# Layer one of a token-pair MLP: both halves of a pair accumulated in one PSUM bank

## The chip, the cores and the metric

The kernel runs on one core of a Trainium2 chip. The metric is the device time of one execution in microseconds (us); three runs of the kernel before are given. The engines in the text are TensorE (PE in the profile, its weight loads PEld), VectorE (DVE), ScalarE (ACT), GpSimd (POOL) and the DMA queue of SyncE (SP).

## The reference

A two-dimensional Fourier transform, of which the real part is kept, followed by two MLPs on the 6016 rows of 256 values:

```
X = fft(fft(x, axis=1), axis=2).real          # x: 2 x 3008 x 256
t = X.reshape(6016, 256)
h = t @ w_in;   t = silu(h) @ w_out           # 256 -> 2048 -> 256
h = t @ w2_in;  out = h * clip(h + 3, 0, 6) / 6 @ w2_out
```

## The kernel before

The real part of the transform at token k and at token -k have the same even part and the opposite odd part over the 256 columns. The kernel therefore works on 3010 pairs: the transform leaves `eo`, an even part (128 rows) and an odd part (128 rows) of each pair, in columns. Layer one multiplies the even part by the folded even weights and the odd part by the folded odd weights; the sum of the two products is the hidden value of one token of the pair, their difference that of the other. Row 0 of the odd part is free of a weight of its own; it holds the value of column 128, the Nyquist term, which enters both tokens alike, and is added by VectorE as `eb` (that row copied to all partitions through DRAM) times `w128_sb`.

All products are of float32 values cut into a high and a low part, three matmuls each (`mm3`, lines 242 to 245): 128 x 128 weights, 502 columns. Layer one runs over six chunks of 502 pairs and sixteen blocks `f` of 128 hidden values, in two passes over the chunks; one chunk and one `f` are a unit, 96 in all, and the first two of them (`EARLY`) are begun while the transform still runs (loop of line 492). Layer two follows with 96 units of its own.

The order on each engine is the order in which the program is written. In the loop of line 597 step i does: `win1` of unit i (six matmuls into the bank pair `ab`; VectorE's reads in lines 471, 474 and 475 make `h`, both tokens), `low` of unit i-1 (GpSimd, line 541: `h` less its high part), `wout1` of unit i-3 (twelve matmuls, line 557, from `ghi` and `glo` into `y00` to `y11`), the low parts of a new chunk that wait in `later` (line 167, `xlo`), and `parts` of unit i (ScalarE, lines 484 and 485: Silu of both tokens, as the high part and in full). Then `spare` lets VectorE go on with other work by a credit of 1150 ns a unit (line 458): the weights arrive as float64 words, and VectorE decodes them in steps (lines 104 to 116, 174 to 180, 142), whose costs in the code are only the credit's counting. `win1` drives this decoder on if the weights of its `f` are not there yet. The last four stretches of that work are the staging of layer two's weights (lines 192 to 202). The bank pair has two buffers, `h` two, `ghi` four, `glo` three.

Of the kernel before, what the change touches and what calls it, by code (L numbers as in the profile page):

```python
# [70 lines left out]
def body(tc, xh, x128, t1, t2, t3, w1, w128, w2, out):  # L71
# [101 lines left out]
    def add_w1(t, a):  # L173
        V.tensor_tensor(out=a[:, :, 0:256], in0=a[:, :, 0:256], in1=t[:, :, 0:256], op=ALU.add)
        yield 680
        V.tensor_tensor(out=t[:, :, 256:512], in0=a[:, :, 256:512], in1=t[:, :, 256:512], op=ALU.add)  # L176
        yield 680
        V.tensor_tensor(out=t[:, :, 0:128], in0=a[:, :, 0:128], in1=a[:, :, 128:256], op=ALU.add)
        yield 420
        V.scalar_tensor_tensor(  # L180
            out=t[:, :, 128:256], in0=a[:, :, 0:128], scalar=mask, in1=a[:, :, 128:256],
            op0=ALU.mult, op1=ALU.subtract,
        )
        yield 420
# [57 lines left out]
    def mm3(o, wh, wl, xhi, xlo, first, last):  # L242
        T.matmul(o, wh, xhi, start=first, stop=False)  # L243
        T.matmul(o, wh, xlo, start=False, stop=False)  # L244
        T.matmul(o, wl, xhi, start=False, stop=last)  # L245
# [274 lines left out]
    def win2(k, f):  # L520
# [4 lines left out]
        hp, h, ghi = hidden_tiles()  # L525
# [71 lines left out]
    for i in range(len(units) + LAG):  # L597
        if i < len(units):
# [176 lines left out]
```

## Time and profile before

| | before |
|---|---|
| median of 3 runs | 989.57 us |
| lowest, highest | 989.51, 989.65 us |
| span of the profiled execution, first to last instruction | 987.7 us |
| mean granted TensorE clock | 0.995 |
| busy: TensorE, VectorE, ScalarE, GpSimd | 972.2, 657.7, 512.3, 234.8 us |

A row of the timeline gives the start in us from the span's start, the duration, the engine, the line, the operation with its output and inputs, and in brackets the idle time of the engine before it and what ended that. Matmuls overlap, so the sum of their durations is more than the time they take; the distance of two starts is what one costs. PEclk is the clock that was granted to TensorE, as a share of 2.4 GHz.

### The profile page before, as it was taken

What the parts mean: (1) busy time and instruction counts of PE and PEld (TensorE: products, weight loads), DVE (VectorE), ACT (ScalarE), POOL (GpSimd) and SP (SyncE); (2) the same over time, 40 slices, a digit from 0 to 9 for tenths busy, and PEclk for the clock granted to TensorE, in tenths of its full rate; (3) what the DMA queues carried; (4) which work ended last, traced back from release to release, by engine and by line L of the source; (5) the groups of instructions that cost most, each with busy time, mean ns of one, the idle gap of its engine ahead of it and who ended that gap; (6) DMA issues with size and microseconds to landing.
All of it is one profiled execution on the core that took longest, in us unless ns stands there. A gap on an engine that the chain in (4) does not pass through costs nothing.

```text
span 987.7 us, 10943 instructions
## 1 busy us (share of the span) xinstructions
PE 972.2 (98%) x4416; PEld 807.9 (82%) x4416; DVE 657.7 (67%) x724; ACT 512.3 (52%) x559; POOL 234.8 (24%) x101
## 2 busy tenths in 40 slices
PE   9979999999899999999999999999999999999998
PEld 8958878888788888888888888888888888888886
DVE  6899999998989765876976455554444444443533
ACT  3867666665465545665555444344443434444442
POOL 0045556565566655552000000000000000000000
PEclk9989999999999999999999999999999999999999
DMA  9411111000212010031100000000000000000000
GB/s 367 170 54 63 54 43 54 11 19 24 75 64 75 23 32 23 31 107 43 43 1 0 1 22 21 21 21 21 0 21 1 21 1 21 11 11 22 1 22 21
DMA packets 11007, 40.46 MB, mean 41 GB/s; under 512 B 1350, under 2 KB 6348, under 8 KB 8140
## 3 DMA queue, kind: packets, MB, share of 16 engines
q1 hardware_dynamic: 10812, 39.49, 11.1%
q8 instruction: 34, 0.56, 0.3%
q10 hardware_dynamic: 144, 0.27, 0.1%
q14 instruction: 17, 0.14, 0.0%
HBM read 31.48 MB, written 8.27 MB: 40 GB/s over the span
## 4 chain that ended last, share of the span: by engine, by line
PE 81%; DVE 13%; issue 3%; ACT 2%; DMA 1%; ACTq 0%; DVEq 0%
PE y L243 14%; PE y L245 14%; PE y L244 14%; PE ab L243 12%; PE ab L245 12%; PE ab L244 12%; DVE h L471 2%; DVE h L474 2%; DVE h L475 2%; DMA x<-in_xh 1%; PE ps L337 1%; PE ps L293 1%; DVE lo L176 1%; DVE wlo L142 1%; DVE lo L116 1%
## 5 line engine op out<-in xcount | busy, mean ns | idle before, releaser
L243 PE MATMUL y<-ghi,whi 128*128 128x502 f32 (+1 forms) x768 | 301.3, 392 | 2.0 <-ACT eo L351 1.7
L245 PE MATMUL y<-ghi,wlo 128*128 128x502 f32 (+1 forms) x768 | 300.7, 392 | 0.0
L244 PE MATMUL y<-glo,whi 128*128 128x502 f32 (+1 forms) x768 | 300.1, 391 | 0.0
L541 POOL TENSOR_TENSOR glo<-h,ghi 128x1004 fp32r<-128x1004 f32 (+1 forms) x96 | 234.4, 2442 | 219.9 <-ACT h L485 191.5
L531 DVE SCALAR_TENSOR_TENSOR h<-h,ab 128x1004 f32<-128x1004 f32 (+1 forms) x96 | 115.2, 1200 | 255.4 <-ACT h L530 255.4
L530 ACT ACTIVATE h<-ab,three 128x1004 f32<-128x1004 f32 (+1 forms) x96 | 105.5, 1099 | 157.0 <-PE ab L245 145.0
L484 ACT ACTIVATE ghi<-h 128x1004 fp32r<-128x1004 f32 (+1 forms) x96 | 100.2, 1044 | 149.8 <-DVE h L475 138.4
L243 PEld LDWEIGHTS y<-ghi,whi 128*128 128x128 f32 x768 | 145.4, 189 | 33.8 <-ACT eo L351 2.4
L244 PEld LDWEIGHTS y<-glo,whi 128*128 128x128 f32 x768 | 145.9, 190 | 30.6
L245 PEld LDWEIGHTS y<-ghi,wlo 128*128 128x128 f32 x768 | 145.2, 189 | 30.2
L482 ACT ACTIVATE ghi<-h 128x1004 fp32r<-128x1004 f32 (+1 forms) x96 | 100.3, 1045 | 125.1 <-DVE h L531 125.1
L243 PE MATMUL ab<-uhi,whi 128*128 128x502 f32 (+1 forms) x384 | 149.9, 390 | 0.0
L245 PE MATMUL ab<-uhi,wlo 128*128 128x502 f32 (+1 forms) x384 | 149.8, 390 | 0.0
L244 PE MATMUL ab<-ulo,whi 128*128 128x502 f32 (+1 forms) x384 | 149.7, 390 | 0.0
L541 DVE TENSOR_TENSOR glo<-h,ghi 128x1004 fp32r<-128x1004 f32 (+1 forms) x96 | 114.9, 1197 | 0.0
L485 ACT ACTIVATE h<-h 128x1004 f32<-128x1004 f32 (+1 forms) x96 | 100.3, 1044 | 9.0 <-ACT ghi L484 0.4
L471 DVE SCALAR_TENSOR_TENSOR h<-eb,w_sb,ab 128x502 f32<-128x502 f32 (+1 forms) x96 | 70.2, 731 | 43.1 <-PE ab L245 38.3
L244 PEld LDWEIGHTS ab<-ulo,whi 128*128 128x128 f32 x384 | 72.6, 189 | 15.2
L243 PEld LDWEIGHTS ab<-uhi,whi 128*128 128x128 f32 x384 | 72.4, 188 | 15.0
L245 PEld LDWEIGHTS ab<-uhi,wlo 128*128 128x128 f32 x384 | 72.2, 188 | 15.0
L243 PE MATMUL ab<-xhi,whi 128*128 128x502 f32 (+1 forms) x192 | 76.1, 396 | 6.2 <-DVE h L475 6.2
L245 PE MATMUL ab<-xhi,wlo 128*128 128x502 f32 (+1 forms) x192 | 75.9, 395 | 1.2 <-DVE wlo L142 1.2
(89 smaller groups left out, 798.8 us busy)
## 6 DMA issues: line engine op xcount, KB each, us to landing
raw<-in_w SPq DMA_DIRECT2D x16, 1024.0 KB, 5.0
x<-in_xh SPq DMA_DIRECT2D x6, 1024.0 KB, 7.0
out<-y SPq DMA_DIRECT2D x20, 251.0 KB, 2.1
eb<-e_d SPq DMA_DIRECT2D x10, 251.0 KB, 3.6
w_d<-ta SPq DMA_DIRECT2D x4, 512.0 KB, 2.9
w<-w_d SPq DMA_DIRECT2D x4, 512.0 KB, 4.1
x<-in_xh SPq DMA_DIRECT2D x3, 512.0 KB
out<-y SPq DMA_DIRECT2D x4, 250.0 KB, 2.0
```

The costliest lines, as they stand in the source:

```text
L243: T.matmul(o, wh, xhi, start=first, stop=False)
L244: T.matmul(o, wh, xlo, start=False, stop=False)
L245: T.matmul(o, wl, xhi, start=False, stop=last)
L471: V.scalar_tensor_tensor(out=h[:, 0, :n], in0=eb[:, :n], scalar=w128_sb[:, f : f + 1], in1=ab[:, 0, :n], op0=ALU.mult, op1=ALU.add)
L474: V.tensor_tensor(out=h[:, 1, :n], in0=h[:, 0, :n], in1=ab[:, 1, :n], op=ALU.subtract)
L475: V.tensor_tensor(out=h[:, 0, :n], in0=h[:, 0, :n], in1=ab[:, 1, :n], op=ALU.add)
L482: A.activation(ghi[:, :, :n], h[:, :, :n], AF.Copy)
L484: A.activation(ghi[:, :, :n], h[:, :, :n], AF.Silu)
L485: A.activation(h[:, :, :n], h[:, :, :n], AF.Silu)
L530: A.activation(h[:, :, :n], hp[:, :, :n], AF.Relu, bias=three)
L531: V.scalar_tensor_tensor(out=h[:, :, :n], in0=h[:, :, :n], scalar=6.0, in1=hp[:, :, :n], op0=ALU.min, op1=ALU.mult)
L541: eng.tensor_tensor(out=glo[:, :, :n], in0=h[:, :, :n], in1=ghi[:, :, :n], op=ALU.subtract)
```

## The change

Layer one's unit is split in two. `win1` now does the even product alone, into one bank (`ab`, four buffers of one bank), and VectorE reads it once: `z` is the bank plus `eb` times `w128_sb`. `win1_end` then accumulates the odd product onto the same bank, without clearing it. The odd weights are folded with the opposite sign, and their row 0 is no longer zero but the weight row 128, so the bank ends as the full hidden value of the second token, Nyquist term included; VectorE computes the first token as twice `z` less the bank. ScalarE takes the second token's Silu from the bank itself. Its two activations over both tokens become four over one each, and GpSimd's subtraction becomes two of half the size. In the loop, step i finishes unit i and then begins unit i+1, both ahead of `low` and `wout1`; a `z` buffer (one) is added. At the start of layer two the pool of the banks is released and a new one of bank pairs is opened. The weight tables follow: `mask` and a new `minus` fold both halves with the same instruction, in place of lines 178 and 180.

```
-        V.tensor_tensor(out=t[:, :, 0:128], in0=a[:, :, 0:128], in1=a[:, :, 128:256], op=ALU.add)
-        V.scalar_tensor_tensor(out=t[:, :, 128:256], in0=a[:, :, 0:128], scalar=mask, in1=a[:, :, 128:256],
-            op0=ALU.mult, op1=ALU.subtract)
+        for o, scalar in ((0, mask), (128, minus)):
+            V.scalar_tensor_tensor(
+                out=t[:, :, o : o + 128], in0=a[:, :, 128 - o : 256 - o], scalar=scalar, in1=a[:, :, o : o + 128],
+                op0=ALU.mult, op1=ALU.add)
+            yield 420
...
     def win1(k, f):
         while len(finished) <= f:
             drive(steps)
-        ab, h, ghi = hidden_tiles()
-        for i in range(2):
-            wh, wl = w(1, f, 128 * i)
-            mm3(ab[:, i, :n], wh, wl, hi[:, i, :n], lo[:, i, :n], True, True)
+        ab = pools[1].tile([P, 512], F32, name="ab", tag="ab")
+        z = pools[0].tile([P, CHUNK], F32, name="z", tag="z", bufs=1)
+        product(ab[:, :n], w(1, f, 0), (hi[:, 0, :n], lo[:, 0, :n]), True)
         V.scalar_tensor_tensor(
-            out=h[:, 0, :n], in0=eb[:, :n], scalar=w128_sb[:, f : f + 1], in1=ab[:, 0, :n], op0=ALU.mult, op1=ALU.add
+            out=z[:, :n], in0=eb[:, :n], scalar=w128_sb[:, f : f + 1], in1=ab[:, :n], op0=ALU.mult, op1=ALU.add
         )
-        V.tensor_tensor(out=h[:, 1, :n], in0=h[:, 0, :n], in1=ab[:, 1, :n], op=ALU.subtract)
-        V.tensor_tensor(out=h[:, 0, :n], in0=h[:, 0, :n], in1=ab[:, 1, :n], op=ALU.add)
-        return h, ghi
+        begun[k, f] = ab, z
+
+    def win1_end(k, f):
+        ab, z = begun.pop((k, f))
+        h, ghi = hidden_tiles()
+        product(ab[:, :n], w(1, f, 128), (hi[:, 1, :n], lo[:, 1, :n]), False)
+        V.scalar_tensor_tensor(
+            out=h[:, 0, :n], in0=z[:, :n], scalar=2.0, in1=ab[:, :n], op0=ALU.mult, op1=ALU.subtract
+        )
+        gs[k, f] = h, ghi, ab
...
-        A.activation(ghi[:, :, :n], h[:, :, :n], AF.Silu)
-        A.activation(h[:, :, :n], h[:, :, :n], AF.Silu)
+        h, ghi, ab = gs[k, f]
+        for s, src in ((1, ab[:, :n]), (0, h[:, 0, :n])):
+            A.activation(ghi[:, s, :n], src, AF.Silu)
+            A.activation(h[:, s, :n], src, AF.Silu)
...
         if g >= 11 and g - 11 < EARLY:
-            k, f = units[g - 11]
-            gs[k, f] = win1(k, f)
-            parts(k, f)
+            win1_end(*units[g - 11])
+            parts(*units[g - 11])
+        if g >= 10 and g - 10 <= EARLY:
+            win1(*units[g - 10])
...
+        if segs[k][0] == 1:
+            for s in (1, 0):
+                G.tensor_tensor(out=glo[:, s, :n], in0=h[:, s, :n], in1=ghi[:, s, :n], op=ALU.subtract)
...
+            if i == n1:
+                pools[1].release()
+                pools[1] = tc.alloc_tile_pool(name="psS", bufs=2, space=PSUM, side="right", reuse_waits="tile")
...
-            if i >= EARLY:
-                gs[k, f] = (win1 if layer == 1 else win2)(k, f)
+                if i >= EARLY:
+                    win1_end(k, f)
+                if EARLY <= i < n1 - 1:
+                    win1(*units[i + 1])
...
-    w1[1:, :, 128:256] = wb[129:256].reshape(P - 1, NF, P)
+    w1[:, :, 128:256] = wb[128:256].reshape(P, NF, P)
```

On TensorE, in the first units, before: `ab_630` is unit 3, both parts, and `y00_644` the start of `wout1` of unit 0.

```order
L243 MATMUL ab_630<-xhi1_530,whi1_0_496 128x502 [waits DVE_49]
L244 MATMUL ab_630<-xlo1_531,whi1_0_496 128x502
L245 MATMUL ab_630<-xhi1_530,wlo1_0_497 128x502
L243 MATMUL ab_630<-xhi1_530,whi1_0_496 128x502
L244 MATMUL ab_630<-xlo1_531,whi1_0_496 128x502
L245 MATMUL ab_630<-xhi1_530,wlo1_0_497 128x502
L243 MATMUL y00_644<-ghi_554,whi1_0_496 128x502 [waits Activation_49]
L244 MATMUL y00_644<-glo_607,whi1_0_496 128x502 [waits Pool_49]
```

Now the even part of unit 3 (`ab_629`), its odd part, the even part of unit 4 (`ab_654`), and then `wout1` of unit 0:

```order
L243 MATMUL ab_629<-xhi1_533,whi1_0_499 128x502
L244 MATMUL ab_629<-xlo1_534,whi1_0_499 128x502
L245 MATMUL ab_629<-xhi1_533,wlo1_0_500 128x502
L243 MATMUL ab_629<-xhi1_533,whi1_0_499 128x502 [waits DVE_49]
L244 MATMUL ab_629<-xlo1_534,whi1_0_499 128x502
L245 MATMUL ab_629<-xhi1_533,wlo1_0_500 128x502
L243 MATMUL ab_654<-xhi1_533,whi1_1_642 128x502 [waits Activation_49]
L244 MATMUL ab_654<-xlo1_534,whi1_1_642 128x502
L245 MATMUL ab_654<-xhi1_533,wlo1_1_643 128x502 [waits DVE_49]
L243 MATMUL y00_663<-ghi_562,whi1_0_499 128x502 [waits PE_49]
L244 MATMUL y00_663<-glo_620,whi1_0_499 128x502 [waits Pool_49]
```

The odd part is a group of its own that waits for VectorE, and a part of unit 4 stands ahead of the first `wout1`.

On VectorE, the same units, before: three reads of `ab` for units 0, 1 and 2, with decode steps of the second weight tile between them.

```order
L471 SCALAR_TENSOR_TENSOR h<-eb_467,w_sb,ab 128x502 [waits DMAHW3_49,PE_49]
L474 TENSOR_TENSOR h<-h,ab 128x502 [waits DVE_49]
L475 TENSOR_TENSOR h<-h,ab 128x502 [waits DVE_49]
L114 TENSOR_SCALAR lo_1_474<-hi_1_473 128x1024
L116 SCALAR_TENSOR_TENSOR lo_1_474<-raw_1_277,lo_1_474 128x1024 [waits DVE_49]
L471 SCALAR_TENSOR_TENSOR h<-eb_467,w_sb,ab 128x502 [waits PE_49]
L474 TENSOR_TENSOR h<-h,ab 128x502 [waits DVE_49]
L475 TENSOR_TENSOR h<-h,ab 128x502 [waits DVE_49]
L174 TENSOR_TENSOR hi_1_473<-hi_1_473,lo_1_474 128x2x256
L176 TENSOR_TENSOR lo_1_474<-hi_1_473,lo_1_474 128x2x256
L178 TENSOR_TENSOR lo_1_474<-hi_1_473 128x2x128 [waits DVE_49]
L180 SCALAR_TENSOR_TENSOR lo_1_474<-hi_1_473,mask 128x2x128
```

Now `h` of one unit and `z` of the next stand together, and the same decode steps (one line number higher) follow:

```order
L484 SCALAR_TENSOR_TENSOR h<-z,ab 128x502 [waits DVE_49,PE_49]
L473 SCALAR_TENSOR_TENSOR z<-eb_470,w_sb,ab 128x502 [waits DVE_49,PE_49]
L115 TENSOR_SCALAR lo_1_477<-hi_1_476 128x1024
L117 SCALAR_TENSOR_TENSOR lo_1_477<-raw_1_280,lo_1_477 128x1024 [waits DVE_49]
L484 SCALAR_TENSOR_TENSOR h<-z,ab 128x502 [waits PE_49]
L473 SCALAR_TENSOR_TENSOR z<-eb_535,w_sb,ab 128x502 [waits DMAHW6_49,DVE_49,PE_49]
L175 TENSOR_TENSOR hi_1_476<-hi_1_476,lo_1_477 128x2x256
L177 TENSOR_TENSOR lo_1_477<-hi_1_476,lo_1_477 128x2x256
L180 SCALAR_TENSOR_TENSOR lo_1_477<-hi_1_476,mask 128x2x128 [waits DVE_49]
L180 SCALAR_TENSOR_TENSOR lo_1_477<-hi_1_476,minus 128x2x128
L484 SCALAR_TENSOR_TENSOR h<-z,ab 128x502 [waits PE_49,Pool_49]
```

Between unit 0's last read and the reads of unit 2 stand the same decode steps as before, while the read that odd(2) needs moved in ahead of four of them.

On VectorE, a unit in the middle of layer one in which the low part of a new chunk (`xlo`) and two decode steps fall, before:

```order
L471 SCALAR_TENSOR_TENSOR h<-eb_801,w_sb,ab 128x502 [waits PE_49,Pool_49]
L474 TENSOR_TENSOR h<-h,ab 128x502 [waits DVE_49]
L475 TENSOR_TENSOR h<-h,ab 128x502 [waits DVE_49]
L167 TENSOR_TENSOR xlo_970<-eo,xhi_969 128x1004 [waits Activation_49]
L174 TENSOR_TENSOR hi_3_767<-hi_3_767,lo_3_768 128x2x256
L176 TENSOR_TENSOR lo_3_768<-hi_3_767,lo_3_768 128x2x256
L471 SCALAR_TENSOR_TENSOR h<-eb_801,w_sb,ab 128x502 [waits PE_49,Pool_49]
L474 TENSOR_TENSOR h<-h,ab 128x502 [waits DVE_49]
L475 TENSOR_TENSOR h<-h,ab 128x502 [waits DVE_49]
```

and now:

```order
L484 SCALAR_TENSOR_TENSOR h<-z,ab 128x502 [waits DVE_49,PE_49,Pool_49]
L473 SCALAR_TENSOR_TENSOR z<-eb_833,w_sb,ab 128x502 [waits DVE_49,PE_49]
L168 TENSOR_TENSOR xlo_1017<-eo,xhi_1016 128x1004 [waits Activation_49]
L175 TENSOR_TENSOR hi_3_796<-hi_3_796,lo_3_797 128x2x256
L177 TENSOR_TENSOR lo_3_797<-hi_3_796,lo_3_797 128x2x256
L484 SCALAR_TENSOR_TENSOR h<-z,ab 128x502 [waits DVE_49,PE_49,Pool_49]
L473 SCALAR_TENSOR_TENSOR z<-eb_833,w_sb,ab 128x502 [waits DVE_49,PE_49]
```

Three steps stand between two pairs of reads as before; the pair behind them is now waited for by the odd part of the next unit.

## Rows read from the trace of the kernel before

**Rows 1.** Page, part 1: busy us (share of span) and instructions of each engine.

```profile
PE 972.2 (98%) x4416; PEld 807.9 (82%) x4416; DVE 657.7 (67%) x724; ACT 512.3 (52%) x559; POOL 234.8 (24%) x101
```

**Rows 2.** Table by stretches (us; busy us and instructions, clock, DMA share, GB/s).

```profile
50.00:75.00 25.00, 19.76 (x78) 14.94 (x77) 24.00 (x31) 17.61 (x20) 12.25 (x5) 0.86 0.16 53
...
250.00:300.00 50.00, 48.12 (x204) 39.53 (x205) 44.92 (x56) 28.07 (x27) 30.05 (x12) 0.97 0.20 69
...
600.00:700.00 100.00, 100.00 (x441) 82.74 (x440) 49.23 (x46) 42.35 (x41) 0.00 (x0) 1.00 0.06 21
```

**Rows 3.** Waits, TensorE: engine, line <- released by: us, times, longest.

```profile
PE ab L243 <- DVE h L475: 6.2, 3, 2.6
```

**Rows 4.** Timeline, TensorE: start, duration (us), line, op [idle before <- releaser].

```profile
125.22 0.50 PE L243 MATMUL ab<-xhi,whi 128*128 128x502 f32 x1 [1.37 <-DVE h L475]
...
131.18 0.49 PE L243 MATMUL y<-ghi,whi 128*128 128x502 f32 x1 [0.22 <-ACT y L563]
...
251.87 0.79 PE L243 MATMUL ab<-xhi,whi 128*128 128x502 f32 x1 [2.57 <-DVE h L475]
252.46 0.62 PE L244 MATMUL ab<-xlo,whi 128*128 128x502 f32 x1
252.88 0.62 PE L245 MATMUL ab<-xhi,wlo 128*128 128x502 f32 x1
```

**Rows 5.** Groups of instructions: count | busy us, mean ns | idle before.

```profile
L541 POOL TENSOR_TENSOR glo<-h,ghi 128x1004 fp32r<-128x1004 f32 (+1 forms) x96 | 234.4, 2442 | 219.9 <-ACT h L485 191.5 <-DVE y L565 7.7 <-DVE ta L200 4.4
...
L484 ACT ACTIVATE ghi<-h 128x1004 fp32r<-128x1004 f32 (+1 forms) x96 | 100.2, 1044 | 149.8 <-DVE h L475 138.4 <-PE y L244 8.0 <-PE ab L245 2.2
...
L471 DVE SCALAR_TENSOR_TENSOR h<-eb,w_sb,ab 128x502 f32<-128x502 f32 (+1 forms) x96 | 70.2, 731 | 43.1 <-PE ab L245 38.3 <-POOL glo L541 4.3 <-issue 0.3
L475 DVE TENSOR_TENSOR h<-h,ab 128x502 f32<-128x502 f32 (+1 forms) x96 | 65.1, 678 | 3.3
...
L563 ACT ACTIVATE y<-y 128x502 f32<-128x502 f32 (+1 forms) x24 | 12.4, 586 | 1.4 <-PE y L245 1.1
```

**Rows 6.** Timeline, VectorE, before GpSimd's first subtraction.

```profile
37.77 1.23 DVE L116 SCALAR_TENSOR_TENSOR lo<-raw,lo 128x1024 f32<-128x1024 uint32 x1
39.03 0.69 DVE L174 TENSOR_TENSOR hi<-hi,lo 128x512 f32<-128x512 f32 x1
...
43.30 0.48 DVE L180 SCALAR_TENSOR_TENSOR lo<-hi,mask 128x256 f32<-128x256 f32 x1
43.69 0.69 DVE L104 TENSOR_SCALAR lo<-lo 128x1024 f32<-128x1024 f32 x1
...
45.23 1.22 DVE L142 TENSOR_TENSOR wlo<-lo,whi 128x1024 fp32r<-128x1024 f32 x1
...
47.83 0.42 DVE L327 TENSOR_TENSOR o<-ps,xr 128x258 f32<-128x258 f32 x1
48.22 1.21 DVE L167 TENSOR_TENSOR xlo<-eo,xhi 128x1004 fp32r<-128x1004 f32 x1
```

**Rows 7.** Timeline, GpSimd and VectorE, two places where they overlap.

```profile
120.16 2.39 POOL L541 TENSOR_TENSOR glo<-h,ghi 128x1004 fp32r<-128x1004 f32 x1 [0.44 <-ACT h L485]
...
120.31 2.79 DVE L106 TENSOR_SCALAR hi<-lo 128x1024 int32<-128x1024 int32 x1
...
245.84 2.82 POOL L541 TENSOR_TENSOR glo<-h,ghi 128x1004 fp32r<-128x1004 f32 x1 [0.70 <-ACT h L485]
...
246.45 3.29 DVE L110 SCALAR_TENSOR_TENSOR ta<-raw,ta 128x1024 int32<-128x1024 int32 x1
```

**Rows 8.** Timeline, TensorE, the first units of layer one.

```profile
46.71 0.39 PE L319 MATMUL ps<-t_sb,out 128*128 128x129 f32 x2
...
56.21 0.49 PE L243 MATMUL ab<-xhi,whi 128*128 128x502 f32 x1 [2.29 <-DVE h L475]
...
59.96 0.79 PE L243 MATMUL y<-ghi,whi 128*128 128x502 f32 x1 [1.73 <-ACT eo L351]
...
67.30 0.39 PE L245 MATMUL ab<-xhi,wlo 128*128 128x502 f32 x1
```

More of the change, by code (lines that the diff above doesn't have):

```diff
@@ L82, in body @@
     mask = per.tile([P, 1], F32, name="mask")
+    minus = per.tile([P, 1], F32, name="minus")
     eo = eop.tile([P, 2, NPAIR], F32, name="eo")
@@ L177, in add_w1 @@
         yield 680
-        V.tensor_tensor(out=t[:, :, 0:128], in0=a[:, :, 0:128], in1=a[:, :, 128:256], op=ALU.add)
[L179 to L184, printed above, removed]
+        for o, scalar in ((0, mask), (128, minus)):
+            V.scalar_tensor_tensor(
+                out=t[:, :, o : o + 128], in0=a[:, :, 128 - o : 256 - o], scalar=scalar, in1=a[:, :, o : o + 128],
+                op0=ALU.mult, op1=ALU.add,
+            )
+            yield 420
     def add_w2(t, a):
@@ L240, in w, with mm3 @@
         return whi[key, g][:, i, c0 : c0 + 128], wlo[key, g][:, i, c0 : c0 + 128]
[L242 to L245, printed above, removed]
+    def mm3(o, wh, wl, xhi, xlo, first, last, **group):
+        T.matmul(o, wh, xhi, start=first, stop=False, **group)
+        T.matmul(o, wh, xlo, start=False, stop=False, **group)
+        T.matmul(o, wl, xhi, start=False, stop=last, **group)
     fft = tc.alloc_tile_pool(name="fft", bufs=1)
@@ L359, in body @@
     V.memset(mask[0:1], 0.0)
+    V.memset(minus, -1.0)
+    V.memset(minus[0:1], 0.0)
     nx = len(XCH)
@@ L450, in hidden_tiles @@
     def hidden_tiles():
-        ps = pools[1].tile([P, 2, 512], F32, name="ab", tag="ab")
         h = pools[0].tile([P, 2, CHUNK], F32, name="h", tag="h", bufs=2)
         ghi = pools[0].tile([P, 2, CHUNK], F32R, name="ghi", tag="ghi", bufs=4)
-        return ps, h, ghi
+        return h, ghi
     def spare():
@@ L460, in spare @@
             advance(steps2, 2000)
+    begun = {}
     def win1(k, f):
@@ L489, in body @@
         tc.alloc_tile_pool(name="wk", bufs=3, side="right", reuse_waits="tile"),
-        tc.alloc_tile_pool(name="psH", bufs=2, space=PSUM, side="right", reuse_waits="tile"),
+        tc.alloc_tile_pool(name="psH", bufs=4, space=PSUM, side="right", reuse_waits="tile"),
     ]
@@ L524, in win2 @@
             drive(steps2)
-        hp, h, ghi = hidden_tiles()
+        hp = pools[1].tile([P, 2, 512], F32, name="hp", tag="hp")
+        h, ghi = hidden_tiles()
         for i in range(2):
@@ L537, in low @@
         n = size(k)
-        h, ghi = gs[k, f]
+        h, ghi = gs[k, f][:2]
         glo = pools[0].tile([P, 2, CHUNK], F32R, name="glo", tag="glo")
-        eng = G if segs[k][0] == 1 else V
-        eng.tensor_tensor(out=glo[:, :, :n], in0=h[:, :, :n], in1=ghi[:, :, :n], op=ALU.subtract)
+        if segs[k][0] == 1:
+            for s in (1, 0):
+                G.tensor_tensor(out=glo[:, s, :n], in0=h[:, s, :n], in1=ghi[:, s, :n], op=ALU.subtract)
+        else:
+            V.tensor_tensor(out=glo[:, :, :n], in0=h[:, :, :n], in1=ghi[:, :, :n], op=ALU.subtract)
         gs[k, f] = ghi, glo
@@ L600, in body @@
             layer, j, fs = segs[k]
-            if i >= EARLY:
-                gs[k, f] = (win1 if layer == 1 else win2)(k, f)
+            if i == n1:
+                pools[1].release()
+                pools[1] = tc.alloc_tile_pool(name="psS", bufs=2, space=PSUM, side="right", reuse_waits="tile")
+            if layer == 2:
+                gs[k, f] = win2(k, f)
+            else:
+                if i >= EARLY:
+                    win1_end(k, f)
+                if EARLY <= i < n1 - 1:
+                    win1(*units[i + 1])
         if 1 <= i <= len(units):
```

7 lines of the change are left out of this document (6 added, 1 removed).

## Prediction

> **What bounds the kernel now.** I read the page first: TensorE is busy for 972.2 of 987.7 us, VectorE for 657.7 [rows 1]. The table by stretches then says where the missing time lies. In layer two (600 to 700 us) TensorE is busy all the time, 441 matmuls in 100 us, so one takes 0.227 us there; no edit to layer one can change that. The stretches of 50 to 75 and 250 to 300 us are short of TensorE time and show a lower granted clock, and VectorE is busy for 24.0 of 25 us in the first [rows 2]. The waits name the cause: three matmuls into `ab` waited 6.2 us in all for line 475, VectorE's last read of the bank pair [rows 3].
>
> So the bound is TensorE, and what can be won is the time in which it waits for VectorE in layer one. A unit there is 18 matmuls, 18 x 0.227 = 4.08 us. Decode steps bear their line numbers of before (one higher in the changed kernel). I call the three matmuls of the even weights even(i), those of the odd weights odd(i), VectorE's new reads of the bank z(i) (line 473 after) and h(i) (line 484 after), and the twelve of line 557 wout(i).
>
> **What can be won in the middle of layer one.** A wait costs its printed idle time and the 0.16 us by which matmuls otherwise overlap (they last 0.39 and start 0.23 apart): 1.37 + 0.16 = 1.5 us at 125.22, 0.22 + 0.16 = 0.4 at 131.18, 2.57 + 0.16 = 2.7 at 251.87. After the last the starts lie 0.42 apart, the 1.2 GHz level, where full speed has 0.23; the row of 250 to 300 us has a mean of 0.97 of full clock, so 3% of 50 us, doubled for half speed, 3 us, were slow, about eight matmuls: 8 x 0.19 = 1.5 us. First matmuls after a wait add 0.2 more [rows 2, 4]. Together 6.3 us. They were VectorE's backlog: three reads of `ab` a unit, 731 + 678 ns and line 474's like 475's [rows 5], against two of about 731 now. That takes 0.62 us off each of 96 units, 60 us of VectorE's 657.7 [rows 1]. Before, a backlog had to pass about 4.7 us to stop TensorE, since the bank pair was wanted again only after twelve, six and twelve matmuls (6.8 us) less 2.1 for the reads. I put this term at **-6.3 us**.
>
> **What the split adds to the path.** odd(i+1) writes the bank that z(i+1) reads, so TensorE now waits for VectorE once more in every unit. From the end of odd(i) VectorE does h(i) and z(i+1), 2 x 0.73 plus gaps, done after 1.53 us if nothing stands before them. TensorE does even(i+1) and wout(i-3) and wants odd(i+1) after some 3.2 us. The slack is therefore about 1.65 us, an estimate from these rows, where it was 4.7. A decode list that runs over the 4.08 us period by more than 1.65 stops TensorE. Behind the waiting odd(i+1) stand even(i+2) and wout(i-2), which nothing lets past.
>
> What decides is how long the decode steps take. Alone they take 0.69 us (lines 104, 174), 0.48 (180) and 1.20 to 1.23 (116, 142, 167) [rows 6]; 106, 114 and 176 I count like the first, 110 like the last. Beside GpSimd they take more: line 106 was issued at 120.31, 0.15 us after a GpSimd subtraction, and took 2.79, to 123.10, about 0.6 past the end of that subtraction; at 245.84 a subtraction was issued while line 106 still ran, and line 110, issued next at 246.45, took 3.29 [rows 7]. So the two take turns, and GpSimd gets in between two VectorE steps. Reads of `ab` don't take part: 731 and 678 are their means over 96 [rows 5]. By the Trainium skill (SBUF — State Buffer, Who interferes with whom) the shared port pair is an exclusive lock and issue order decides who blocks; by that rule every overlap is paid in full, which is the upper end of both terms below, and those rows agree. GpSimd's 2442 ns [rows 5] in two halves I take as 1.2 us each. By the Trainium skill (GPSIMD Engine Reference, Elementwise — side-by-side cycle accounting) two-input work costs about 2.6 cycles an element plus a dispatch that each instruction pays; a half would then cost an estimated 1.28 us, and the sum would be about 1 us longer.
>
> The halves also move. Before, GpSimd began after both activations of a unit (1.04 each [rows 5]), late enough to run partly beside the three reads of the next. Now its first half can begin after two activations of half the size, some 1.1 us behind h(i), just when VectorE starts to decode.
>
> **The first units, worked through.** In the program's order TensorE now has odd(3) and even(4) ahead of wout(0), where it had wout(0) ahead of both parts of unit 4; VectorE has each z behind the h before it, with the same decode steps between. Start: even(0) stands where line 319's matmuls began at 46.71 [rows 8] and ends at 47.6; z(0) ends at 48.4 (VectorE idles 0.9 before it). Then line 110 (49.55), the add of line 327 (0.42 [rows 6], 49.95), xlo (51.05), h(0) 51.8, z(1) 52.55. Line 114 ends at 53.2, where GpSimd's first half takes its turn to 54.4, line 116 ends at 55.6, h(1) 56.35, z(2) 57.1. Line 174 57.75, a half to 58.95, line 176 59.6, a half to 60.8, the two small ones (178, 180) to 61.65, h(2) 62.4, z(3) 63.1. ScalarE follows h(2) with four activations (2.1 us, at a spacing somewhat under the 586 ns of one of this size [rows 5]) and the copy to whi (as line 484, 1.04): 65.55. wlo waits out another half and ends at 68.1. Only then can even(4) end, wout(0) run to 71.1 and odd(4) to 71.8. In the trace of before the same point (units 0 to 4 and wout(0) all issued) is 67.30 + 0.23 = 67.53, although two waits of 2.29 and 1.73 us lie ahead of it [rows 8]. So +4.3 us. Without any blocking the same list gives 66.8: -0.7 us. Rows 7 lie near the blocked end, and a few halves will fall beside reads of `ab`: I take **+4.0**.
>
> The clock: before, the starts around 59.96 lie in a slow spell, and the stretch's granted mean is 0.86 [rows 2, 8]. The new chain has waits of over 2 us before odd(2), odd(3) and the end of even(4); the restart at 251.87 ran slow for eight matmuls [rows 4]. If wout(0) runs slow after its wait, that costs 8 x 0.19 = **+1.5** (0 to 1.9).
>
> **New waits later.** Most units have one or two decode steps and stay inside the slack: 1.53 + 1.22 + 1.2 + 1.22 = 5.2, 1.1 over the period. Eight units have three or four: two with xlo, 174 and 176, one with xlo, 180, 104 and 106, one with xlo, 176 and 178, four of the staging with 104, 106 and 110. For the first kind 1.53 + 1.21 + 0.69 + 0.68 and two halves make 6.5, 2.4 over, so TensorE would wait 0.8; with a third half left over from the unit ahead, 1.9. Ends: 0, if the halves miss them, and 8 us, if all eight are hit at about 1 us each. I take 1.5 for each of the two of the first kind, **+3.0**, since their three steps all want the port, and nothing for the others.
>
> **Hidden.** ScalarE's halves cost it 0.2 us more a unit in a stretch where it is busy for 28 of 50 us [rows 2]. GpSimd's result is wanted three units later, 12 us. The four `ab` banks come free two units before they are wanted, at the change to layer two also. Two memsets at the start lie beside the first loads. Without those covers each would cost its duration.
>
> **Sum.** -6.3 + 4.0 + 1.5 + 3.0 = +2.2. The profiled execution's span is 987.7, so 989.9; the median of the runs, 989.57, stands 1.9 above that span, and I add the difference to it: 991.8. By the bounds: -6.3 - 0.7 = -7.0 (982.6) to -6.3 + 4.3 + 1.9 + 8 = +7.9 (997.5).
>
> **Rivals.** (1) VectorE's relief reaches TensorE: halves make the blocking short, nothing new waits, the first units come out even. -6.3 - 0.7 + 1.0 = -6.0: 983.6. For it: 60 us less work on the engine that TensorE waited for. Against it: rows 7, and the slack that falls from 4.7 to 1.65. It holds if the steps after GpSimd's halves take under 1 us. (2) The halves pile up on all eight long lists: +7.9, 997.5. It decides once a list of three steps meets three halves. (3) The waits only change place: the first units lose 4.0, full clock soon after, one later wait of 1.5: -0.8, 988.8; faster than before by less than can be told.
>
> **How the numbers follow.** A measurement of this kernel can tell about 0.2%, 2.0 us, from no change. Forecast (989.6 to 995) 0.50, of which 0.20 lie under 991.6; rival 3 0.12; rival 1 0.20; rival 2 0.18. So faster 0.20, same 0.32, slower 0.48. For 8 in 10 the range leaves out about half of rival 1 and the end of rival 2: 985.5 to 997.
>
> **What would show it.** Right: in the first 75 us a wait of TensorE for line 473 before odd(3) of over 3 us, and wout(0) starting near 68, not at 59.96; no wait near the old 125 and 250 us; new waits for line 473 where VectorE's list has xlo, 174 and 176; VectorE's busy time down by some 50 to 60 us. Wrong: if steps such as line 176 stay near 0.7 us beside GpSimd, rival 1 holds; if TensorE waits for 473 in many units of two steps, the slack is smaller than I reckon, and the time passes 997.

## The result, and the profile after

| | before | after |
|---|---|---|
| median, us | 989.54 | 996.3 |
| single executions, us | 989.47 to 989.65 | 994.24, 996.11, 996.48, 996.49 |
| profiled execution, us (its span) | 989.57 (987.7) | 994.24 (992.5) |
| TensorE idle in the span, us | 15.5 | 17.5 |

The ratio is 1.0064, with an interval of 1.0049 to 1.0078: the kernel became slower by 0.6%, 6.8 us. The prediction said 991.8 us and slower, with a range of 985.5 to 997.0. The direction holds and the time lies in the range, but near its upper end and above the 989.6 to 995 that the likeliest case was given.

The page of after, busy time of each engine, answers to [rows 1]:

```profile
PE 975.0 (98%) x4416; PEld 807.4 (81%) x4416; DVE 571.0 (58%) x630; ACT 525.1 (53%) x751; POOL 255.7 (26%) x197
```

VectorE lost 87 us of work, and TensorE needs 2.8 us more for as many matmuls. The table by stretches says where, beside [rows 2]; its columns are busy time and instructions of PE, PEld, DVE, ACT and POOL, then granted clock, DMA share and GB/s:

```profile
50.00:75.00 25.00, 16.57 (x57) 11.73 (x56) 20.24 (x22) 14.05 (x24) 12.22 (x8) 0.73 0.16 52
...
250.00:300.00 50.00, 50.00 (x220) 41.22 (x219) 34.14 (x43) 30.10 (x53) 32.90 (x26) 1.00 0.20 69
600.00:700.00 100.00, 100.00 (x438) 82.20 (x437) 49.30 (x46) 42.47 (x42) 0.00 (x0) 1.00 0.06 21
```

The first stretch got worse (57 matmuls instead of 78, clock 0.73 instead of 0.86), the stretch of 250 to 300 us is healed, and layer two, whose matmuls the change leaves as they were, does 438 matmuls in 100 us where it did 441. The waits of TensorE and its timeline, against [rows 3, 4, 8]:

```profile
PE ab L243 <- DVE z L473: 9.9, 5, 3.4
...
PE ab L245 <- DVE wlo L143: 0.9, 1, 0.9
PE ab L243 <- ACT whi L158: 0.7, 1, 0.7
```

```profile
52.44 0.49 PE L243 MATMUL ab<-xhi,whi 128*128 128x502 f32 x1 [0.80 <-DVE z L473]
56.68 0.50 PE L243 MATMUL ab<-xhi,whi 128*128 128x502 f32 x1 [2.60 <-DVE z L473]
62.18 0.79 PE L243 MATMUL ab<-xhi,whi 128*128 128x502 f32 x1 [3.38 <-DVE z L473]
64.55 0.79 PE L243 MATMUL ab<-xhi,whi 128*128 128x502 f32 x1 [0.75 <-ACT whi L158]
66.66 0.79 PE L245 MATMUL ab<-xhi,wlo 128*128 128x502 f32 x1 [0.90 <-DVE wlo L143]
67.24 0.62 PE L243 MATMUL y<-ghi,whi 128*128 128x502 f32 x1
67.66 0.62 PE L244 MATMUL y<-glo,whi 128*128 128x502 f32 x1
...
71.81 0.38 PE L243 MATMUL ab<-xhi,whi 128*128 128x502 f32 x1
```

```profile
119.12 0.49 PE L243 MATMUL ab<-xhi,whi 128*128 128x502 f32 x1 [1.91 <-DVE z L473]
```

```profile
149.41 0.49 PE L243 MATMUL ab<-xhi,whi 128*128 128x502 f32 x1 [1.25 <-DVE z L473]
```

odd(1), odd(2) and odd(3) wait for z, even(4) for its weights, wout(0) starts at 67.24 at the 0.42 us spacing of half speed, and later only two units wait. Nothing waits near 125, 131 and 251 us.

To turn this into a sum, number the matmuls of 500 or 502 columns in both traces, from 0, and compare the start of number k (a count of the trace's rows, not a view):

| matmul k | start in after, us | after minus before, us |
|---|---|---|
| 60 | 76.6, first units over | +4.9 |
| 150 | 97.2 | +5.0 |
| 450 | 169.4, both new waits passed | +6.7 |
| 1000 | 295.0, the old wait at 251.87 passed | +2.0 |
| 1728 | 461.4, about where layer two begins | +2.3 |
| 4031 | last | +4.7 |

So the first units cost 4.9 us, the middle gave 2.9 back, the rest of layer one added 0.3, and layer two 2.4 in small change: 2,303 matmuls, 1.05 ns each (they start 228.86 ns apart instead of 227.81). The other executions are another 2 us longer, at a mean granted clock of 0.989 to 0.990 against 0.993.

Beside [rows 5], the groups of after (count, busy us, mean ns, idle before):

```profile
L560 POOL TENSOR_TENSOR glo<-h,ghi 128x502 fp32r<-128x502 f32 x160 | 213.8, 1358 | 175.9 <-PE y L244 97.7 <-ACT h L501 78.2
...
L473 DVE SCALAR_TENSOR_TENSOR z<-eb,w_sb,ab 128x502 f32<-128x502 f32 x80 | 59.1, 738 | 10.0 <-PE ab L245 1.5
L484 DVE SCALAR_TENSOR_TENSOR h<-z,ab 128x502 f32<-128x502 f32 x80 | 54.1, 677 | 105.1 <-PE ab L245 94.5 <-issue 6.7 <-POOL glo L560 3.6
...
L177 DVE TENSOR_TENSOR lo<-hi,lo 128x512 f32<-128x512 f32 x7 | 8.7, 1247 | 0.0
```

A GpSimd half takes 1.36 us, so two take more than the 2.44 of a whole one. The first of the two later waits, in the timeline of VectorE and then of GpSimd (as [rows 7]; x2 means both halves in one row):

```profile
112.73 1.53 DVE L168 TENSOR_TENSOR xlo<-eo,xhi 128x1004 fp32r<-128x1004 f32 x1 [1.40 <-ACT xhi L167]
114.18 1.76 DVE L175 TENSOR_TENSOR hi<-hi,lo 128x512 f32<-128x512 f32 x1
115.87 1.75 DVE L177 TENSOR_TENSOR lo<-hi,lo 128x512 f32<-128x512 f32 x1
117.54 0.67 DVE L484 SCALAR_TENSOR_TENSOR h<-z,ab 128x502 f32<-128x502 f32 x1
118.32 0.74 DVE L473 SCALAR_TENSOR_TENSOR z<-eb,w_sb,ab 128x502 f32<-128x502 f32 x1
```

```profile
113.73 3.34 POOL L560 TENSOR_TENSOR glo<-h,ghi 128x502 fp32r<-128x502 f32 x2 [0.53 <-ACT h L501]
```

Lines 175 and 177 take 1.76 and 1.75 us beside the two halves of 113.73 to 117.07, where line 174 before took 0.69 without such company [rows 6]; z(15) ends at 119.06 and odd(15) starts at 119.12. The wait at 149.41 is odd(22), behind a list of the same kind; just ahead of that list, h(20) had stood for 1.25 us, at the end for GpSimd, which still read the buffer of `h` that h(20) was to fill.

### The profile page after: what moved, and what is told of

Read it like the earlier page. It is cut to its first block, busy times and chain, and to the rows that moved or that the text cites. A ratio compares the mean times of both kernels' runs of the same rounds, so it can differ in the third digit from the quotient of the medians.

```text
span 992.5 us, 11053 instructions
## 1 busy us (share of the span) xinstructions
PE 975.0 (98%) x4416; PEld 807.4 (81%) x4416; DVE 571.0 (58%) x630; ACT 525.1 (53%) x751; POOL 255.7 (26%) x197
## 4 chain that ended last, share of the span: by engine, by line
PE 92%; DVE 2%; ACT 0%; issue 0%; DVEq 0%
PE y L245 18%; PE y L243 17%; PE y L244 17%; PE hp L245 9%; PE hp L243 9%; PE hp L244 9%; PE ab L245 4%; PE ab L243 4%; PE ab L244 4%; DVE lo L177 0%; DVE hi L175 0%; DVE z L473 0%; DVE h L484 0%; DVE lo L180 0%; DVE wlo L143 0%
## 5 line engine op out<-in xcount | busy, mean ns | idle before, releaser
L560 POOL TENSOR_TENSOR glo<-h,ghi 128x502 fp32r<-128x502 f32 (+1 forms) x192 | 255.3, 1351 | 199.5 <-PE y L244 116.9
L549 DVE SCALAR_TENSOR_TENSOR h<-h,hp 128x1004 f32<-128x1004 f32 (+1 forms) x96 | 115.2, 1200 | 259.3 <-ACT h L548 259.3
L548 ACT ACTIVATE h<-hp,three 128x1004 f32<-128x1004 f32 (+1 forms) x96 | 105.5, 1099 | 160.9 <-PE hp L245 150.2
L496 ACT ACTIVATE ghi<-h 128x1004 fp32r<-128x1004 f32 (+1 forms) x96 | 100.3, 1045 | 125.1 <-DVE h L549 125.1
L245 PE MATMUL hp<-uhi,wlo 128*128 128x502 f32 (+1 forms) x384 | 150.7, 392 | 0.0
L243 PE MATMUL hp<-uhi,whi 128*128 128x502 f32 (+1 forms) x384 | 150.1, 391 | 0.0
L244 PE MATMUL hp<-ulo,whi 128*128 128x502 f32 (+1 forms) x384 | 149.9, 390 | 0.0
L244 PEld LDWEIGHTS hp<-ulo,whi 128*128 128x128 f32 x384 | 72.7, 189 | 15.8
L243 PEld LDWEIGHTS hp<-uhi,whi 128*128 128x128 f32 x384 | 72.3, 188 | 15.3
L245 PEld LDWEIGHTS hp<-uhi,wlo 128*128 128x128 f32 x384 | 72.2, 188 | 15.2
```

The costliest lines, as they stand in the source:

```text
L243: T.matmul(o, wh, xhi, start=first, stop=False, **group)
L244: T.matmul(o, wh, xlo, start=False, stop=False, **group)
L245: T.matmul(o, wl, xhi, start=False, stop=last, **group)
L548: A.activation(h[:, :, :n], hp[:, :, :n], AF.Relu, bias=three)
L549: V.scalar_tensor_tensor(out=h[:, :, :n], in0=h[:, :, :n], scalar=6.0, in1=hp[:, :, :n], op0=ALU.min, op1=ALU.mult)
L560: G.tensor_tensor(out=glo[:, s, :n], in0=h[:, s, :n], in1=ghi[:, s, :n], op=ALU.subtract)
```

## The experiments

Every time is a median, and every ratio stands against the kernel before on the same chip.

| run | what differs | us (executions) | ratio to before, interval |
|---|---|---|---|
| 1 | after, constants share a tile | 991.16 (10) | 1.0024, 1.0014 to 1.0033 |
| 2 | before, plus 32 unused bytes | 992.73 (5) | 1.0036, 1.0021 to 1.0050 |
| 3 | after, no GpSimd subtraction | 986.8 (7) | 0.9971, 0.9960 to 0.9982 |
| 4 | run 1, subtraction whole | 996.4 (4) | 1.0069, 1.0054 to 1.0084 |
| 5 | run 1, even parts two ahead | 987.93 (10) | 0.9984, 0.9975 to 0.9993 |
| 6 | run 1, wout(0) before even(4) | 989.8 (10) | 1.0003, 0.9994 to 1.0012 |
| 7 | run 1, subtraction on VectorE | 985.69 (5) | 0.9960, 0.9946 to 0.9974 |
| 8 | before, subtraction on VectorE | 1003.56 (2) | 1.0139, 1.0121 to 1.0158 |
| 9 | before, no GpSimd subtraction | 980.51 (2) | 0.9909, 0.9891 to 0.9927 |
| 10 | run 7 with run 6's move | 983.9 (5) | 0.9944, 0.9930 to 0.9957 |
| 11 | run 10, less decoding before z(3) | 982.61 (5) | 0.9933, 0.9921 to 0.9946 |
| 12 | after again | 996.44 (4) | 1.0070, 1.0053 to 1.0087 |

### Why layer two is slower: 32 bytes (runs 1 and 2)

Layer two's matmuls, their order and their banks are the same before and after, but the new constant `minus` is a tile of its own ahead of the weights, and it shifts them: the first weight tile starts at byte 16,640 of each partition before and at 16,672 after. Run 1 takes the shift away from after:

```
-    mask = per.tile([P, 1], F32, name="mask")
-    minus = per.tile([P, 1], F32, name="minus")
+    signs = per.tile([P, 2], F32, name="signs")
+    mask, minus = signs[:, 0:1], signs[:, 1:2]
```

> The changed kernel, with its new constant (the column of -1) no tile of its own but the second column of the tile that holds the other constant. A tile of one float takes 32 bytes of each partition here and stands ahead of the weights, so in the changed kernel all weight tiles lie 32 bytes further than before; in this one they lie where they lay before. The work and its order are the same. Theory 'shift' (the weights' place costs the 1.05 ns by which the matmuls of layer two are further apart after, 228.86 against 227.81 ns): spacing in layer two back at 227.8, layer two 2.4 us shorter, the whole 2.4 to 3.5 us under the changed kernel (991 to 994 us), waits at 56, 62, 119 and 149 us unchanged. Rival 'elsewhere' (the accumulation, PSUM's banks or the execution itself): spacing 228.9, time as the changed kernel's, 994 to 996.5.

Run 2 gives the shift, and nothing else, to before: the lines that make and fill `minus`, which nothing reads.

> The kernel before with one unused tile of 32 bytes a partition, written twice at the start, ahead of the weights: the weights lie 32 bytes further, as after the change. Theory 'shift': spacing in layer two 228.9 instead of 227.8 ns, about 4,030 matmuls by 0.3 to 1.05 ns, 991.5 to 993.5 us. Rival 'elsewhere': 227.8 and 989.6 us.

Layer two in the table by stretches, run 1 first, then run 2:

```profile
600.00:700.00 100.00, 100.00 (x441) 82.78 (x440) 49.27 (x46) 43.17 (x42) 0.00 (x0) 1.00 0.06 21
```

```profile
600.00:700.00 100.00, 100.00 (x438) 82.31 (x437) 49.47 (x47) 43.25 (x42) 0.00 (x0) 1.00 0.06 21
```

441 and 438 have changed sides with the 32 bytes. In run 1 the k-th matmul stands 3.60 us behind before's at the start of layer two and 3.60 at its end, where after drifts by 2.4. Run 2 is 3.2 us slower than before, 0.75 of it in layer one and 2.4 in layer two; run 1 is faster than after by 3.7 if the fastest executions are compared (990.54 against 994.24; 3.4 against the 993.95 of run 12) and by 5.1 in the median, which also counts that fewer of its executions were long ones. Theory "shift" holds. Which of the tiles that move with it counts is not shown: the weights, the raw words and `y1` moved together, and of these TensorE reads the weights alone. Only two places were tried, so how the cost goes with the offset is open.

Run 1's profiled execution (993.15) also shows what the longer executions of this order have. After its wait of 1.95 us at 119.68 it went on at half speed:

```profile
119.68 0.49 PE L243 MATMUL ab<-xhi,whi 128*128 128x502 f32 x1 [1.95 <-DVE z L473]
...
120.61 0.62 PE L243 MATMUL ab<-xhi,whi 128*128 128x502 f32 x1
121.02 0.62 PE L244 MATMUL ab<-xlo,whi 128*128 128x502 f32 x1
```

The starts lie 0.41 us apart for eight matmuls; in after's profiled execution the same wait of 1.91 us was followed by full speed. That spell is worth 1.5 us (eight by 0.19), and the early one is longer too. At the 300th matmul run 1 stands 2.1 us behind after, about what separates after's executions from one another.

### Whether the longer executions of after are the same thing (run 12)

> The changed kernel once more, unaltered: its profiled execution took 994.24 us, the three others 996.1 to 996.5, and their mean granted clock was 0.989 to 0.990 against 0.993. Theory 'second spell' (in most executions the wait for line 473 near 119 us is followed by a spell of half speed of 3.4 us, as in the first and fourth run, and the early spell is longer): a profiled execution of 996 us shows half speed after 119 us, the two worth 2 us; one of 994 us shows none. Rival 'elsewhere': a slow spell at another place, after 149 us or in layer two.

The four executions took 993.95 to 996.54, and the one with a profile was the shortest; it has no second spell, as expected of a short one. So the second spell is seen in runs 1 and 4, which have after's order, and is only argued for after's own 996 us.

### What GpSimd's turns cost, after and before (runs 3 and 9)

```
-            for s in (1, 0):
-                G.tensor_tensor(out=glo[:, s, :n], in0=h[:, s, :n], in1=ghi[:, s, :n], op=ALU.subtract)
+            glo = ghi
```

> The changed kernel without GpSimd's subtractions (the low parts of layer one's hidden values aren't made, the matmuls that read them read the high parts again, as many columns in the same time). Theory 'turns' (VectorE's decode steps between two of its reads of the bank are stretched by GpSimd's halves, and TensorE waits behind them): VectorE's lines 117, 177, 180, 107 and 143 early are 1.2, 1.2, 0.48, 0.69 and 1.2 us instead of 2.17, 1.77, 1.47, 1.64 and 1.69, so the chain to the first product of unit 0 comes 3.5 to 4.5 us earlier and the waits for line 473 at 119 and 149 us are gone: 985 to 989 us. Rival 'order' (the even part of unit 4 before the first product, and z before the odd part, cost the time whatever GpSimd does): early waits of the same sum to 1 us, 992 to 995.

> The kernel before without GpSimd's subtractions (low parts of layer one's hidden values not made, the high parts read twice). It prices GpSimd's turns before the change, as the third run priced them after it (9.5 us). Theory 'turns': the waits at 66.5, 125.2, 131.2 and 251.9 us are VectorE steps stretched by GpSimd, and go: 1.2 + 1.4 + 0.2 + 2.6 us and the slow clock of 1.7 us after the last, 7 us in all, 981.5 to 984.5. Rival 'order before': the three reads of the bank in a row are late by themselves, half of it stays, 985.5 to 988.

Both runs leave out the low parts of the hidden values. Run 3 took 9.5 us less than after and run 9 took 9.0 less than before (7.1 and 9.2 between the profiled executions; after's median is one of its longer ones). Waits of TensorE for z in run 3, then the page of run 9 and its waits for `h`:

```profile
PE ab L243 <- DVE z L473: 3.3, 3, 1.6
```

```profile
PE 968.2 (99%) x4416; PEld 806.5 (82%) x4416; DVE 606.9 (62%) x724; ACT 514.1 (53%) x559; POOL 0.4 (0%) x5
```

```profile
PE ab L243 <- DVE h L475: 2.3, 1, 2.3
```

In run 9 the waits at 66.5, 125.2, 131.2 and 251.9 us are all gone, and two early ones stay. Rival "order before" falls, and the gain went past the expected 7: three reads of the bank a unit fit beside TensorE when nobody takes turns with VectorE. In run 3 the waits at 119 and 149 us are gone, the three early ones shrink from 6.8 to 3.3 us, and VectorE's busy time is 544.0 us. wout(0) starts at 64.75, 2.5 us earlier than in after, where 3.5 to 4.5 were expected, but layer one's first matmul also came 1.1 us later in this execution (47.73 against 46.67). One thing the two runs do not part from the turns: without the subtractions VectorE also never waits for GpSimd to free a buffer of `h` (3.6 us of its idle time in after, in the row of line 484 above, 4.3 before [rows 5]). The same group of line 177 in run 3, against 1247 ns above:

```profile
L473 DVE SCALAR_TENSOR_TENSOR z<-eb,w_sb,ab 128x502 f32<-128x502 f32 x80 | 59.0, 738 | 10.7 <-PE ab L245 1.9 <-DVE h L484 0.5
...
L177 DVE TENSOR_TENSOR lo<-hi,lo 128x512 f32<-128x512 f32 x7 | 4.8, 684 | 0.0
```

The decode step falls to 684 ns, z stays at 738 to the nanosecond: a VectorE instruction that reads the bank takes no part in the turns, as the prediction assumed. By the Trainium skill (SBUF — State Buffer, Who interferes with whom) only VectorE's dual-port modes and instructions with two SBUF inputs contend with GpSimd; these two groups agree.

Without GpSimd the changed kernel (986.8, or 983.6 with run 2's 3.2 us taken off, an estimate) is slower than the kernel before without it (980.5). So the split and its order cost some 3 us by themselves, and run 3's rival "order" is right to that extent: at matmul 60 the two traces already stand 3.2 us apart.

### Halves or a whole (run 4)

```
-            for s in (1, 0):
-                G.tensor_tensor(out=glo[:, s, :n], in0=h[:, s, :n], in1=ghi[:, s, :n], op=ALU.subtract)
+            G.tensor_tensor(out=glo[:, :, :n], in0=h[:, :, :n], in1=ghi[:, :, :n], op=ALU.subtract)
```

> The kernel of the first run here (shared constant), with GpSimd's subtraction of a unit in one instruction over both halves again. Theory 'turns': a whole one holds VectorE up for as long in sum (2.35 us against 1.35 twice); the waits for line 473 are 1 to 2 us longer at 62 and 119 us, the time 0 to +3 us against the first run. Rival 'halves cost' (two instructions per unit take the port twice, and the second half is what VectorE meets): waits at 62 and 119 us 1 us shorter, time 1 to 2 us less.

Waits of TensorE in run 4, and the one of odd(15):

```profile
PE ab L243 <- DVE z L473: 11.6, 7, 3.3
```

```profile
120.96 0.79 PE L243 MATMUL ab<-xhi,whi 128*128 128x502 f32 x1 [3.01 <-DVE z L473]
```

Against run 1 the wait of odd(15) grew from 1.95 to 3.01, that of odd(3) from 2.61 to 3.31, and two new ones came at 162 and 187 us (0.20 and 0.97); that of odd(2) shrank from 2.60 to 1.66. The direction is as expected; 5.2 us in the median is more than the 0 to 3 expected. VectorE's busy time is nearly the same (573.3 us against 570.5 in run 1): the whole subtraction costs it no more in sum, but more at the one step that z waits behind. The trace of run 4 shows where: lines 168, 175 and 177, the steps ahead of z(15), take 2.59, 2.84 and 0.68 us beside two whole ones, against 1.52, 1.77 and 1.76 beside halves in run 1, 1.06 us more together. The halves are a part of the change that helps.

### The two later waits (run 5)

```
...
-                if EARLY <= i < n1 - 1:
-                    win1(*units[i + 1])
+            for u in range(nxt[0], min(i + 3, n1)):
+                ku, fu = units[u]
+                if u > i + 1 and (not 6 < u <= FAR or ku != units[i + 1][0] and (ku not in xs or later) or len(finished) <= fu):
+                    break
+                win1(ku, fu)
+                nxt[0] = u + 1
```

> The kernel of the first run (after with the shared constant, 991.16 us), with the even part of units 7 to 28 begun two units ahead instead of one where the unit's list and weights are there (a second z lies in columns of y1 that are first written after unit 33). Units 0 to 6 go as they did. Theory 'z late' (the waits at 119.68 and 151.50 us, 1.95 and 1.26 us, are odd parts that stand behind z, and z behind xlo and decode steps in GpSimd's turns): both waits gone, with the slow clock of 3.4 us after the first; the spots of slow clock before 73 us unchanged; 991.16 minus 3.2 to 5 = 986.2 to 988. Rival 'throughput' (VectorE is behind in sum in these units, so the wait only moves to the next odd part or to an even part): waits of 1 to 2 us within two units of the old places, 990 to 991.

Of all waits after 73 us one is left in run 5:

```profile
115.06 0.49 PE L244 MATMUL ab<-xlo,whi 128*128 128x502 f32 x1 [0.29 <-DVE xlo L168]
```

3.2 us less in the median, as expected of "z late". VectorE keeps up in sum; what was short was the slack of one z.

### The first units (run 6)

```
-                if EARLY <= i < n1 - 1:
+                if EARLY <= i < n1 - 1 and i != 3:
...
             (wout1 if segs[k_][0] == 1 else wout2)(k_, f_)
+            if i == 3:
+                win1(*units[4])
```

> The kernel of the first run (991.16 us), with one thing moved: the even part of unit 4 stands behind the first product (the twelve matmuls of unit 0 into y) instead of ahead of it. Theory 'order early' (after the change TensorE waits at 64.71 and 66.81 us for unit 4's weights with the twelve matmuls ready behind them, which before stood ahead): the first product starts at 63.5 to 64.5 us instead of 67.3, the waits of 0.75 and 0.90 us vanish, odd(4) waits 0.5 to 1.2 us for its z instead; net -1.5 to -2.5 us: 988.7 to 989.7. Rival 'VectorE bound early' (what is late is VectorE's chain of decode steps up to unit 5's weights, whatever TensorE does in between): the gain is given back at the next unit, 990.5 to 991.5.

```profile
62.34 0.79 PE L243 MATMUL ab<-xhi,whi 128*128 128x502 f32 x1 [3.12 <-DVE z L473]
...
63.76 0.62 PE L243 MATMUL y<-ghi,whi 128*128 128x502 f32 x1
...
69.96 0.49 PE L243 MATMUL ab<-xhi,whi 128*128 128x502 f32 x1 [0.83 <-DVE z L473]
```

In this timeline of run 6 wout(0) starts at 63.76, both waits for weights are gone and odd(4) pays 0.83 for its z. The gain is 1.4 us in the median, a little under the 1.5 expected at least. So the order that put even(4) ahead of wout(0) carries about 1.4 us of the early cost, and the rest stays in the waits for z at 56 and 62 us.

### Where the freed VectorE time can be spent (runs 7, 8, 10, 11)

Run 7, and for before run 8, put the subtraction on VectorE:

```
-            for s in (1, 0):
-                G.tensor_tensor(out=glo[:, s, :n], in0=h[:, s, :n], in1=ghi[:, s, :n], op=ALU.subtract)
+            V.tensor_tensor(out=glo[:, :, :n], in0=h[:, :, :n], in1=ghi[:, :, :n], op=ALU.subtract)
```

> The kernel of the first run (991.16 us), with layer one's subtraction on VectorE (one instruction over both halves, as layer two has it) and GpSimd idle. VectorE gets 96 x 1.22 us = 117 us more work, and loses what GpSimd's turns cost it. Theory 'turns' (the run without the subtractions was 9.5 us faster than the changed kernel, of which each early subtraction on VectorE gives back 1.2 us, three before the first product): early chain 2 to 3 us shorter, waits near 119 and 151 us gone: 984 to 987.5 us. Rival 'VectorE full' (z, h, the subtraction, a decode step and the share of xlo are 0.73 + 0.68 + 1.22 + 1.2 + 0.3 = 4.1 us for a unit, as long as its 18 matmuls at 228 ns): waits for line 473 in many units up to 230 us, 995 to 1003 us.

> The kernel before (989.54 us), with layer one's subtraction on VectorE. Theory 'room' (what the change gives is time on VectorE, which before has none to spare beside the decode steps: 0.73 + 0.68 + 0.68 + 1.22 + 1.2 + 0.3 = 4.8 us a unit against 4.1 of TensorE): TensorE waits in most units between 130 and 230 us and again behind the accumulators' copies, 995 to 1005 us, so the same edit has opposite signs before and after. Rival 'turns only' (GpSimd's turns cost before more than the subtraction would): 982 to 988 us.

The page of run 7 with its waits for z, the page of run 8, then the first waits of TensorE in run 8:

```profile
PE 969.9 (99%) x4416; PEld 805.1 (82%) x4416; DVE 647.3 (66%) x726; ACT 525.6 (53%) x751; POOL 0.4 (0%) x5
```

```profile
PE ab L243 <- DVE z L473: 4.3, 3, 1.9
```

```profile
PE 977.0 (98%) x4416; PEld 808.2 (81%) x4416; DVE 708.9 (71%) x820; ACT 512.9 (51%) x559; POOL 0.4 (0%) x5
```

```profile
PE y L243 <- DVE y L565: 5.8, 3, 3.5
PE y L243 <- ACT y L563: 3.7, 3, 1.7
PE ab L243 <- DVE h L475: 3.0, 2, 2.3
```

One edit, opposite signs: 5.5 us faster after the change, 14 slower before it. After the change VectorE's 647 us leave room and no turn is lost: the three waits for z that are left all lie before 61 us. Before, with 709 us of work, it is late for the copies of line 565 that free the accumulators (5.8 us); another 3.7 us are waits for ScalarE's copies of line 563. The time fits theory "room", its place only in part: between 130 and 230 us TensorE waits at four places, not in most units. So of these two kernels the edit pays in the changed one alone; the reads and the banks changed together, and how much each of them gives is not shown.

Run 10 adds run 6's move to run 7. Run 11 also cuts the decode steps ahead of z(3):

```
-        advance(steps, 1700 if g < 8 else 1400)
+        advance(steps, 1700 if g < 8 else 1400 if g < 13 else 400)
```

> The seventh run's kernel (shared constant, subtraction on VectorE, 985.69 us) with the sixth's move (even part of unit 4 behind the first product, worth 1.4 us there). Theory 'separate': the two gains add, since the waits at 62.92 and 64.71 us (0.75 and 0.59) still stand ahead of the first product in the seventh: 983.5 to 985. Rival 'VectorE bound early': with the subtractions of units 0 to 2 in VectorE's queue its chain up to unit 5's weights sets the end, 985.3 to 986.

> The tenth run's kernel with 400 instead of 1400 credit for decode steps in the last turn of the transform, so that fewer of them stand ahead of z(3). Theory 'z behind steps': the wait for odd(3) at 60.5 us is 0.4 to 1 us shorter, and unit 4's weights come no later, since VectorE's work up to them is the same: -0.3 to -1 us against the tenth run. Rival 'weights bound': what is gained before odd(3) is lost at unit 4's weights, no change within 0.3 us.

```profile
59.74 0.79 PE L243 MATMUL ab<-xhi,whi 128*128 128x502 f32 x1 [1.09 <-DVE z L473]
61.16 0.62 PE L243 MATMUL y<-ghi,whi 128*128 128x502 f32 x1
```

In run 11 odd(3) starts at 59.74 and wout(0) at 61.16, against 62.18 and 67.24 in after. Both gains add to run 7's (1.8 and 1.3 us, the second somewhat over its expected 1). Run 11, 982.61 us, beats before by 6.9 us (0.67%) and after by 13.7.

## Why the prediction was right in direction, and where it was off

**The term that goes, -6.3 us: right in size, half right in cause.** All three waits went. The middle gave 2.9 us back net of 3.5 of new waits, so about 6.4 left. But the prediction laid the backlog to three reads of the bank a unit. Run 9 keeps them and loses the waits: without GpSimd's turns there is no backlog, and what the change did was to give VectorE the time to bear them.

**The first units, +4.0 and +1.5: right in mechanism, 0.6 us too much.** The chain came as worked through, with each list some half a microsecond shorter: z(2) ended at 56.6 (57.1 worked out), z(3) at 62.1 (63.1), wlo at 66.6 (68.1), though a half took 1.36 us and not 1.2. wout(0) began at 67.24, and the wait before odd(3) was 3.38. The clock of 0.73 over 25 us is 13.5 us at half speed, against 7.0 before.

**New waits, +3.0: 3.5 measured, at the two lists named.** odd(15) and odd(22), behind the lists with xlo, 174 and 176, wait by 1.91 and 1.25 us (plus 0.16 each), and nothing waits behind the other six long lists. Run 5 shows the slack of one z to be the reason. Not foreseen: ahead of the first, VectorE comes so early that it waits 1.40 us for ScalarE's `xhi`, and loses time that it had won.

**The step that failed: "no edit to layer one can change that", said of layer two.** An edit to the constants did. The two memsets were costed (beside the first loads, rightly nothing), their tile's 32 bytes were not: 2.4 us in layer two, 3.2 us in all by run 2. Forecast 991.8, plus 3.2, is 995.0; the rest to 996.3 fits the second slow spell that three in four executions seem to have. The terms that were forecast come to -6.4 + 4.9 + 3.5 = +2.0 in the profiled execution, against +2.2; that they meet so closely is in part luck, since the first units were put 0.6 too high and the new waits 0.5 too low. And the time lies in the range only because that was left wide for rival 2, whose mechanism did not come.

**VectorE, -87 us against 50 to 60.** Without GpSimd the two kernels differ by 606.9 - 544.0 = 62.9 us, the 60 of the removed reads. The other 24 are turns: they cost VectorE 50.8 us before (657.7 - 606.9) and 27.0 after (571.0 - 544.0). It isn't the halves, since run 4 with the whole subtraction loses 29.3. That a VectorE without a backlog meets GpSimd less often is likely, and only argued. A half took 1.36 us, not 1.2, so two of them are longer than the 2.44 of a whole one, which by itself would have cost VectorE more, not less.

**The rivals.** Rival 1 (983.6) fell on the slack and on the first units. Rival 2's 997.5 is near the measured time, but its mechanism, all eight long lists late, did not come: two were. Rival 3 had full clock soon after the first units' waits and one later wait: wout(0) ran at half speed from its start, and two units wait later.

## What to carry to other kernels

When an edit takes work off an engine that is not the bound, ask which wait ends last and who makes it: here some 9 us of the medians hung on GpSimd before and after, and the freed VectorE time paid only once it was spent on taking GpSimd's work over. An edit that makes a bound engine wait for another once more per step needs as much slack as that engine's longest list of other work, or one more buffer. And a new small tile ahead of large ones moves all of them: compare the spacing of the matmuls in a stretch whose code did not change.

## What was not expected of the hardware

- Weight tiles, with what lies behind them, 32 bytes further in SBUF (16,672 instead of 16,640 bytes from the partition's start): layer two's matmuls of 500 or 502 columns start 228.86 instead of 227.81 ns apart (after and run 2 against before and run 1), and go back when the tiles do.
- Waits of the same length on TensorE (1.91 us at 119.12 in after, 1.94 at 117.27 in run 6, 1.95 at 119.68 in run 1) were followed by full speed in after and run 6 and by 3.4 us at 1.2 GHz in run 1. Why is not shown.
- GpSimd's turns cost VectorE 50.8 us of busy time before the change and 27 to 29 after it, and the kernel 9.0 and 9.5 us in the medians (9.2 and 7.1 between the profiled executions): half the busy time, and most of the kernel's time still. So the sum of the turns does not tell what they cost the end; who waits behind the held-up step does.
